# Attention denominators from q's sketch for every chunk but the first, and another queue for the load of S2

## The chip, the cores and the metric

The kernel runs on one core of a Trainium2 chip. The metric is the device time of one execution in microseconds. The engines of the core are called PE (TensorE), DVE (VectorE), ACT (ScalarE), POOL (GpSimd) and SP (SyncE); SP only issues transfers here. Each engine works through its own list of instructions, and waits for the others by semaphores.

## The reference

Two layers follow one another: an attention with a polynomial sketch in place of the softmax, and a feed-forward layer with a squared relu.

```python
def phi(x):                                   # S1, S2: 8 x 32
    a = np.einsum('rd,bhsd->bhsr', S1, x)
    b = np.einsum('rd,bhsd->bhsr', S2, x)
    return np.einsum('bhsi,bhsj->bhsij', a, b).reshape(*x.shape[:-1], 64)
q_p, k_p = phi(q), phi(k)                     # q, k, v: 4 x 4 x 1088 x 32
kv = np.einsum('bhsf,bhsd->bhfd', k_p, v)
z = np.sum(k_p, axis=2)
num = np.einsum('bhsf,bhfd->bhsd', q_p, kv)
den = np.einsum('bhsf,bhf->bhs', q_p, z)[..., None] + 1e-06
x = (num / den)                               # heads side by side: 4352 x 128
h = np.maximum(x @ w_in, 0.0)                 # w_in: 128 x 2048
out = h * h @ w_out                           # w_out: 2048 x 128
```

The denominator is a sum over 64 features of q, but those are products a_i b_j of two sketches of 8 numbers each. So it can be written as the sum over i of a_i times (sum over j of z_ij b_j). The second factor is a sketch of q with its own matrix, S2 weighted by z, of 8 rows again: 8 products in place of 64.

## The kernel before, in words

The work is cut by batch (b = 0 to 3). In each batch, the list `AC` cuts the attention of q into chunks, given as a first group of tokens and a count of groups; batch 0 has three, (0, 8), (8, 12) and (20, 16), and each later batch one. The list `FC` cuts the feed-forward layer into column ranges: 256, 384 and 448 for batch 0. The feed-forward layer runs in units. A unit is one to two blocks of 128 hidden features of one column range: `ffn1` (L610) multiplies x by a block of w_in into the PSUM tile pg, `relu` takes it to SBUF on ACT, `square` squares it on ACT or DVE, and `ffn2` (L637) multiplies by w_out and sums into the PSUM tile po. The first two units hold one block each, the rest of that range two. w_in is rounded on POOL by `cast_wi`, a quarter (four blocks) at a time.

Everything before L815 is the prologue, whose order is the program's own. SP and ACT issue the loads. A DVE transpose of the loaded S1 and S2 (s_nat to s_T, L706) feeds the copies to sf and sq, the sketch matrices. `a_kT0` transposes k, `a_kf` sketches it on PE, `a_kp0` forms the products on DVE, and `a_kv0` sums kv and z on PE into the PSUM tile kvp. The first chunk of q (256 columns) is then made by itself: q0 sketches it into x0, and qp0 is its product. bd is kvp set out in blocks, one half for the denominator and one for the numerator; den0 and num0 are the matmuls with it, and dT, rd, bc and xT on DVE divide one by the other. kvt is a copy of kvp; `a_rep` replicates it by four matmuls with the constant irep, and kv (and z0) are taken from there for the later chunks of batch 0. `keep_warm` issues matmuls whose result isn't used.

Everything after L815 is ordered by a planner, `_Order`. Each task is given its engine, a planned length, a key (a due time) and what it needs; the planner runs through planned time, always taking the ready task of smallest key on a free engine, and writes the instructions out in that order. PSUM has one tile called att for qc, nd, kc and kvp in turn.

For a later chunk, `a_qT` transposes q on DVE, `a_qc` sketches it on PE, `a_qs` spreads the sketches over the features on DVE (qb, qa), `a_qp` multiplies them, `a_nd` multiplies by kv on PE, `a_bc` and `a_x` divide on DVE. Where the denominators come from differs. In batch 0, `a_nd` has further matmuls with z (L547) and `a_dn` turns their rows into reciprocals. In batches 1 to 3, `a_w` (L453) has put the z-weighted sketch matrix into columns 16 to 23 of sw, so `a_qc` yields the weighted sketch beside the others. `a_qt` transposes qc on DVE, `a_pd` multiplies the two sketches, `a_rc` sums and inverts, and `a_rl` moves the results to the partitions that need them by 16 small copies on POOL.

Of the kernel before, what the change touches and what calls it, by code (L numbers as in the profile page):

```python
# [9 lines left out]
F32 = mybir.dt.float32  # L10
# [94 lines left out]
def kernel(  # L105
# [21 lines left out]
    W0, W3 = 10, 3  # L127
# [37 lines left out]
    z0 = sb("z0", 64 * H)  # L165

# [48 lines left out]
    nc.scalar.dma_start(s_nat[8:16, :], S2[:, :])  # L215
# [10 lines left out]
    for p in range(4):  # L226
        load_v(nc.sync, 0, p, 4, NT)
    load_wi(nc.sync, 0)
    load_wi(nc.sync, 1)
    load_q(nc.sync, 0, 256, S)  # L230
# [22 lines left out]
    own_c, own_p = sb("own_c", 32), sb("own_p", 2)  # L253
    nc.vector.memset(own_c[:], 0.0)
# [3 lines left out]
    for h in range(H):  # L258
        nc.vector.memset(own_c[32 * h : 32 * h + 32, 8 * h : 8 * h + 8], 1.0)
# [170 lines left out]
    def a_rep_z(t_, col):  # L430
        nc.vector.tensor_tensor(
            out=_ap(z0, 0, 128, 0, [[32, 4], [128, 2], [1, 32]]),
            in0=_ap(t_, 0, 128, col + 32, [[512, 4], [64, 2], [1, 32]]),
            in1=_ap(own_c, 0, 128, 0, [[0, 4], [0, 2], [1, 32]]),
            op=mult,
        )

# [10 lines left out]
    def a_qc(b, i0, nb):  # L448
        st[b, "qc", i0] = att("qc")
        sketch(st[b, "qc", i0], qT, 32 * i0, 8 * nb, sw[b % 2] if b else sf[:, 64:96])  # L450
# [14 lines left out]
    def a_qt(b, x):  # L465
        if x == 0:
            st[b, "qt"] = wpool.tile([128, 32 * NT * H], F32, tag="qt", bufs=1, name="qt")
        m = 32 * NT
        nc.vector.transpose(  # L469
            _ap(st[b, "qt"], 0, 128, 2 * m * x, [[m, 2], [1, m]]),  # L470
            banks(st[b, "qc", 0], 2 * x, 0, m),
        )

    def a_pd(b):
        qt = st[b, "qt"]
        nc.vector.tensor_tensor(
            out=_ap(pd, 0, 128, 0, [[9, 4 * NT], [1, 8]]),
            in0=_ap(qt, 0, 128, 0, [[32, 4 * NT], [1, 8]]),
            in1=_ap(qt, 0, 128, 16, [[32, 4 * NT], [1, 8]]),
            op=mult,  # L480
        )


    def a_rc(b):
        dn = wpool.tile([128, 4 * NT], F32, tag="dn", name="dn")
        nc.vector.tensor_reduce(
            out=dn[:, :], in_=_ap(pd, 0, 128, 0, [[9, 4 * NT], [1, 9]]), op=add, axis=AX
        )
        st[b, "rc"] = wpool.tile([128, 4 * NT], F32, tag="rc", bufs=1, name="rc")
        nc.vector.reciprocal(st[b, "rc"][:, :], dn[:, :])  # L490


    def a_rl(b, c):
        if c == 0:
            st[b, "rd", 0] = wpool.tile([128, 4 * NT], F32, tag="rd", name="rd")
        for h in range(H):
            nc.gpsimd.tensor_copy(  # L497
                st[b, "rd", 0][32 * h : 32 * h + 32, NT * c : NT * c + NT],
                st[b, "rc"][32 * c : 32 * c + 32, NT * h : NT * h + NT],
            )  # L500
# [26 lines left out]

    def a_nd(b, i0, nb, nd=None, col=0):
        m = 8 * nb
        nd = att("nd") if nd is None else nd  # L530
        st[b, "nd", i0] = nd, col
        kv, z = st[b, "kv"], z0
        for e in range(E):
            qp = st[b, "qp", i0, e]
            ch = [(c, h) for c in range(4) for h in range(H)]
            for c, h in ch:
                r, o = slice(32 * c, 32 * c + 32), 64 * h + 32 * e
                nc.tensor.matmul(  # L538
                    nd[32 * h : 32 * h + 32, 512 * c + col : 512 * c + col + m],
                    kv[r, o : o + 32], qp[r, m * h : m * h + m],  # L540
                    start=(e == 0), stop=(e == 1),
                )
        for o_, m0, w in dens(m) if b == 0 else ():
            for e in range(E):
                for h in range(H):
                    o = 64 * h + 32 * e
                    nc.tensor.matmul(  # L547
                        nd[32 * h : 32 * h + 32, col + o_ : col + o_ + w],
                        z[:, o : o + 32], st[b, "qp", i0, e][:, m * h + m0 : m * h + m0 + w],
                        start=(e == 0), stop=(e == 1),  # L550
                    )

    def dens(m):
        return [(m, 0, m)]

    def a_dn(b, i0, nb):
        m = 8 * nb
        (nd, col), q4 = st[b, "nd", i0], nb // 4
        dT = wpool.tile([128, 32 * NT], F32, tag="dT", bufs=1, name="dT")
        for o_, m0, w in dens(m):  # L560
            nc.vector.transpose(dT[:, m0 : m0 + w], nd[:, col + o_ : col + o_ + w])
        dn = wpool.tile([128, 4 * NT], F32, tag="dn", name="dn")
        nc.vector.tensor_scalar(
            out=_ap(dn, 0, 128, 0, [[q4, 4], [1, q4]]),
            in0=_ap(dT, 0, 128, 0, [[8, 4], [32, q4]]),
            scalar1=1e-6, scalar2=None, op0=add,
        )
        rd = st[b, "rd", i0] = wpool.tile([128, 4 * NT], F32, tag="rd", name="rd")
        nc.vector.reciprocal(rd[:, 0:nb], dn[:, 0:nb])
# [10 lines left out]
    def a_x(b, i0, nb, x, k=2):  # L580
        m = 8 * nb
        if (b, "xT") not in st:
            st[b, "xT"] = bpool.tile([128, SP], F32R, tag="xT", name="xT")
        nc.vector.tensor_tensor(  # L584
            out=_ap(st[b, "xT"], 0, 128, 32 * i0 + 2 * m * x, [[m, k], [1, m]]),
            in0=banks(st[b, "nd", i0][0], 2 * x, st[b, "nd", i0][1], m, k),
            in1=_ap(st[b, "bc", i0], 0, 128, 2 * m * x, [[m, k], [1, m]]),
            op=mult,
        )
# [137 lines left out]
    iden, irep = sb("iden", 128), sb("irep", 128)  # L727
    make_identity(nc, iden[:])
# [27 lines left out]
    a_kf(4, 3, psf, "po")  # L756
    q0(0)
# [3 lines left out]
    for t0, n in ((0, 2), (2, 2), (4, 3), (7, 2)):  # L761
        a_kp0(t0, n)
        for t in range(t0, t0 + n):
            a_kv0(t)
        if t0 == 0:
            a_kf(7, 2, psf, "po")
# [5 lines left out]
    for y in range(2):  # L772
        nc.tensor.matmul(  # L773
            den0[64 * y : 64 * y + 64, 0:256], eps[0:1, 0:64], eps[0:1, 64:320],
            start=True, stop=False,
        )

    bd = sb("bd", 256)
    for x in (1, 0):
# [5 lines left out]
        )  # L785
    st["kvt"] = wpool.tile([128, 128], F32, tag="kvt", name="kvt")
    nc.scalar.copy(st["kvt"][:, :], st[0, "kvp"][:, 0:128])
# [5 lines left out]
    for t_, x in ((den0, 1), (num0, 0)):  # L793
        for y in range(2):
            nc.tensor.matmul(  # L795
                t_[64 * y : 64 * y + 64, 0:256], bd[:, 128 * x + 64 * y : 128 * x + 64 * y + 64],
                qp0[:, 256 * y : 256 * y + 256], start=(x == 0), stop=True,
            )
    a_rep(x0, 256)
    st["warm"] = psf.tile([128, 512], F32, tag="po", name="warm")  # L800
    keep_warm(W3)
    a_rep_kv(x0, 256)
# [10 lines left out]
    a_rep_z(x0, 256)  # L813
# [26 lines left out]
    def q_tasks(b, i0, nb, key):  # L840
# [4 lines left out]
        if True:  # L845
            for x in range(2):
# [7 lines left out]
                )  # L854
        O.add(
            ("qc", b, i0), {"PE": 0.75}, k0 - 1.0, names + [("w", b)], on(a_qc, b, i0, nb),
            rings=[("att", 1)], lag=PEL,
        )
        prev["qTuse"] = [("qc", b, i0)] if i0 + nb == 4 * NT else []
        if b:  # L860
            for x in range(2):
                O.add(
                    ("qt", b, x), {"DVE": dve(m)}, k0 - 0.3 + 0.1 * x, [], on(a_qt, b, x),
                    uses=[("qc", b, i0)], rings=[("qt", 1)] if x == 0 else [],
                )
            O.add(
                ("pd", b), {"DVE": dve(m // 2)}, k0 - 0.1, [("rc", b - 1)], on(a_pd, b),
                uses=[("qt", b, 0), ("qt", b, 1)],
            )
            O.add(  # L870
                ("rc", b), {"DVE": 0.8}, k0 - 0.1, [], on(a_rc, b), uses=[("pd", b)],
                rings=[("rc", 1)],
            )
            for c in range(4):
                O.add(
                    ("rl", b, c), {"POOL": 0.8}, k0 + 0.1 * c, [], on(a_rl, b, c),
                    uses=[("rc", b)], rings=[("rd", 2)] if c == 0 else [],
                )
# [16 lines left out]
    def nd_tasks(b, i0, nb, key):  # L895
# [3 lines left out]
            ("nd", b, i0), {"PE": 1.65 if b else 0.7 + 2.5 * max(nb, 14) / 36}, key - 3.5 - 4 * dve(m), [("kvr", b, h) for h in range(H)], on(a_nd, b, i0, nb),  # L899
            uses=qps + [("qp", b, i0, 0, 0)], rings=[("att", 1)], lag=PEL,  # L900
        )
        if b == 0:
            O.add(
                ("dn", b, i0), {"DVE": 0.72 + m / 960 / 2}, key - 3.0 - 4 * dve(m), [],
                on(a_dn, b, i0, nb), uses=[("nd", b, i0)],
            )
        for x in range(2):
            O.add(
                ("bc", b, i0, x), {"DVE": dve(m)}, key - 2.5 - 4 * dve(m) + 0.1 * x, [], on(a_bc, b, i0, nb, x),
                uses=[("dn", b, i0)] if b == 0 else [("rl", b, 2 * x), ("rl", b, 2 * x + 1)],  # L910
# [88 lines left out]
    for u in range(NU):  # L999
# [8 lines left out]
        for i in range(m):  # L1008
# [13 lines left out]
            tu[u] - 0.6, [],  # L1022
# [65 lines left out]
```

## Time and profile before

| what | value |
|---|---|
| median of 8 runs | 189.24 us (189.12 to 195.46) |
| the profiled execution's own time | 189.18 us |
| its span, first to last instruction | 187.4 us |
| PE busy | 181.8 us, 97% |
| ACT busy | 149.5 us, 80% |
| DVE busy | 114.9 us, 61% |
| POOL busy | 28.0 us, 15% |
| bytes moved | 11.27 MB, mean 60 GB/s |

The profile is that of one execution. Its span is 1.78 us shorter than the time, since something lies before the first instruction and after the last. The busy time of PE includes the time in which a matmul's result is still on its way, so a busy PE need not be full. A line of the timeline has the start in us from the span's begin, the length in us, the engine, the line of the kernel, the operation, its output and inputs, the shape and the count, and in brackets the idle time before it with what ended that. SPq and ACTq are the instructions that issue transfers; PEld are weight loads.

### The profile page before, as it was taken

How to read it: one execution, taken by the hardware profiler on the slowest of the kernel's cores; microseconds unless marked ns; L12 is line 12 of the kernel's file. 1: busy time of each engine (PE TensorE's matmuls, PEld its weight loads, DVE VectorE, ACT ScalarE, POOL GpSimd, SP SyncE). 2: the span in 40 equal slices, each digit the busy share in tenths (PEclk: the TensorE clock that was granted, in tenths of full speed). 3: DMA queues.
4: the chain of work that ended last, by engine and by line, in shares of the span. 5: the costliest groups of instructions: out<-in, count | busy, mean ns of one | idle time of the engine just before them, and what ended most of it. 6: DMA issues, size and time to landing. Idle time of an engine off the chain costs nothing.

```text
span 187.4 us, 4142 instructions
## 1 busy us (share of the span) xinstructions
PE 181.8 (97%) x1586; PEld 121.8 (65%) x1587; DVE 114.9 (61%) x261; ACT 149.5 (80%) x329; POOL 28.0 (15%) x125
## 2 busy tenths in 40 slices
PE   8999999999999999999999999999999999999991
PEld 2757866666656666656577666656577655666890
DVE  4779879958992589469944589469943412222400
ACT  3418778778978989789698989789698998999960
POOL 2841000028400000085000000085000000000000
PEclk9999999999999999999999999999999999999997
DMA  5799600100039600200069200200020200020101
GB/s 184 185 346 305 151 3 2 28 3 5 0 51 242 155 3 0 44 1 2 7 140 257 35 3 0 42 3 0 7 41 0 35 0 2 9 43 0 32 11 28
DMA packets 24411, 11.27 MB, mean 60 GB/s; under 512 B 17864, under 2 KB 22728, under 8 KB 24392
## 3 DMA queue, kind: packets, MB, share of 16 engines
q1 hardware_dynamic: 23940, 10.82, 23.9%
q8 instruction: 12, 0.20, 0.4%
q10 hardware_dynamic: 452, 0.20, 0.4%
q14 instruction: 7, 0.06, 0.1%
HBM read 8.78 MB, written 2.23 MB: 59 GB/s over the span
## 4 chain that ended last, share of the span: by engine, by line
PE 94%; DMA 2%; DVE 1%; issue 0%; ACT 0%; POOL 0%; ACTq 0%; DVEq 0%
PE po L653 60%; PE pg L615 18%; PE nd L538 3%; PE kvp L394 2%; PE pol L648 2%; PE po L648 2%; PE qc L296 2%; DMA s_nat<-in_S_dram 2%; PE kvp L376 1%; PE kf L306 1%; PE kc L296 1%; PE x L749 1%; PE nd L547 1%; PE den L795 0%; PE den L773 0%
## 5 line engine op out<-in xcount | busy, mean ns | idle before, releaser
L653 PE MATMUL po<-g,w_o 128*128 128x384 f32 (+3 forms) x352 | 138.4, 478 | 0.0
L615 PE MATMUL pg<-xT,w_in 128*128 128x384 f32 (+3 forms) x192 | 110.1, 582 | 0.3 <-DVE xT L810 0.3
L624 ACT ACTIVATE gt<-pg 128x384 f32<-128x384 f32 (+4 forms) x177 | 85.3, 490 | 19.9 <-PE pg L615 16.9
L653 PEld LDWEIGHTS po<-g,w_o 128*128 128x128 f32 x352 | 62.6, 189 | 22.3 <-issue 7.3
L632 ACT ACTIVATE g<-gt 128x384 f32<-128x384 f32 (+3 forms) x138 | 71.1, 532 | 2.9
L615 PEld LDWEIGHTS pg<-xT,w_in 128*128 128x128 f32 x192 | 36.0, 190 | 25.1 <-issue 6.0
L634 DVE TENSOR_TENSOR g<-gt 128x384 f32<-128x384 f32 (+4 forms) x39 | 21.3, 549 | 39.5 <-ACT gt L624 39.4
L443 POOL COPY kv<-kvt 32x64 f32<-32x64 f32 x48 | 11.8, 246 | 90.5 <-PE po L653 63.9
L506 DVE STREAM_SHUFFLE qa<-qc 128x576 f32<-128x576 f32 (+2 forms) x20 | 11.6, 653 | 0.0
L521 DVE TENSOR_TENSOR qp<-qa,qb 128x576 f32<-128x576 f32 (+2 forms) x20 | 10.8, 607 | 0.0
L497 POOL COPY rd<-rc 32x9 f32<-32x9 f32 x48 | 8.9, 185 | 2.1
L347 DVE TENSOR_TENSOR kp<-fs 128x576 f32<-128x576 f32 x12 | 8.2, 739 | 0.0
L469 DVE STREAM_TRANSPOSE qt<-qc 128x576 f32<-128x576 f32 x6 | 4.3, 761 | 5.6 <-PE qc L296 5.6
L657 DVE STREAM_TRANSPOSE oT<-po 128x384 f32<-128x384 f32 (+3 forms) x11 | 6.2, 562 | 1.2 <-PE po L653 1.0
L538 PE MATMUL nd<-qp,kv 32*32 32x288 f32 (+2 forms) x320 | 6.8, 353 | 0.0
L338 DVE STREAM_TRANSPOSE fs<-kc 128x576 f32<-128x576 f32 x6 | 4.3, 761 | 3.9 <-PE kc L296 3.9
L538 PEld LDWEIGHTS nd<-qp,kv 32*32 32x32 f32 x320 | 3.8, 103 | 3.5 <-issue 2.1
L584 DVE TENSOR_TENSOR xT<-nd,bc 128x576 fp32r<-128x576 f32 (+2 forms) x10 | 5.6, 596 | 0.8 <-PE nd L538 0.7
L506 DVE STREAM_SHUFFLE qb<-qc 128x576 f32<-128x576 f32 (+2 forms) x10 | 6.0, 647 | 0.0
L289 DVE STREAM_TRANSPOSE qT<-qn 128x192 f32<-128x192 f32 (+3 forms) x11 | 5.8, 561 | 0.0
L696 PE MATMUL warm<-const-bfloat16-1.0 128*128 128x512 bf16 x12 | 4.9, 561 | 0.8 <-PEq L1072 0.8
L575 DVE STREAM_TRANSPOSE bc<-rd 128x576 f32<-128x576 f32 (+2 forms) x10 | 5.7, 609 | 0.1
(98 smaller groups left out, 97.6 us busy)
## 6 DMA issues: line engine op xcount, KB each, us to landing
kn<-in_k_dram SPq DMA_DIRECT2D x3, 544.0 KB, 7.0
qn<-in_q_dram SPq DMA_DIRECT2D x3, 544.0 KB, 7.0
vn<-in_v_dram SPq DMA_DIRECT2D x9, 144.0 KB, 5.7
out_dram<-oT SPq DMA_DIRECT2D x24, 48.0 KB, 1.8
w_in<-in_moe_w_in_dram SPq DMA_DIRECT2D x4, 256.0 KB, 5.4
w_o<-in_moe_w_out_dram SPq DMA_DIRECT2D x4, 256.0 KB, 5.2
out_dram<-oT SPq DMA_DIRECT2D x8, 56.0 KB, 1.9
qn<-in_q_dram SPq DMA_DIRECT2D x1, 416.0 KB, 4.8
```

The lines of the kernel that those rows point to most:

```text
L347: nc.vector.tensor_tensor(out=_ap(st[b, "kp"], 0, 128, 2 * o, [[64, NT], [8, 8], [1, 8]]), in0=_ap(fs, 0, 128, o, [[32, NT], [1, 8], [0, 8]]),
L443: nc.gpsimd.tensor_copy(_ap(st[b, "kv"], 32 * c, 32, 64 * h, [[32, E], [1, 32]]), _ap(st["kvt"], 32 * h, 32, 0, [[64, E], [1, 32]]),)
L497: nc.gpsimd.tensor_copy(st[b, "rd", 0][32 * h : 32 * h + 32, NT * c : NT * c + NT], st[b, "rc"][32 * c : 32 * c + 32, NT * h : NT * h + NT],)
L506: nc.vector.stream_shuffle(in_=banks(st[b, "qc", i0], 2 * x, 0, m), out=_ap(st[b, which, i0], 0, 128, 2 * m * x, [[m, 2], [1, m]]), mask=m ...
L521: nc.vector.tensor_tensor(out=st[b, "qp", i0, e][:, r], in0=st[b, f"qa{e}", i0][:, r], in1=st[b, "qb", i0][:, r], op=mult,)
L538: nc.tensor.matmul(nd[32 * h : 32 * h + 32, 512 * c + col : 512 * c + col + m], kv[r, o : o + 32], qp[r, m * h : m * h + m], start=(e == 0 ...
L615: nc.tensor.matmul(st["pg", u][:, n * i : n * i + n], w_in[:, 128 * (d0 + i) : 128 * (d0 + i) + 128], st[b, "xT"][:, c0 : c0 + n],)
L624: nc.scalar.activation(gt[:, 0:w], st["pg", u][:, 0:w], Relu)
L632: nc.scalar.activation(g2[:, 0:w], gt[:, 0:w], Square)
L634: nc.vector.tensor_tensor(out=g2[:, 0:w], in0=gt[:, 0:w], in1=gt[:, 0:w], op=mult)
L648: nc.tensor.matmul(po[x // 128][:, 0:128], g[:, x : x + 128], w, start=(d == 0), stop=(d == NB - 1),)
L653: nc.tensor.matmul(po[0][:, 0:n], w, g, start=(d == 0), stop=(d == NB - 1))
```

## The change

It has these parts.

- The denominators of batch 0's second and third chunks are made as those of batches 1 to 3 are. The matmuls with z, `a_dn`, `a_rep_z`, z0 and own_c go. `a_qt`, `a_pd`, `a_rc` and `a_rl` take the chunk's first group and count, and the planner gives these tasks to every chunk after the first.
- The weighted sketch matrix of batch 0 is made in the prologue: own_f is a mask summed from the identity, zm is z with that mask, s2f is S2 transposed, and four small matmuls give columns 16 to 23 of sw, which ACT copies out of x0.
- The sketch qc of the second chunk, and its two transposes of q, go from the planner into the prologue; the load of q is cut at column 640, and its first part stands ahead of w_in's.
- S2 is the first load on SP's queue; S1 alone stays on ACT's.
- The last of the four sketches of k comes before the kv matmuls and not between them; kvt is copied by DVE; the replicas come before num0; the identity is made earlier on POOL. The matmuls of `keep_warm` there are one and one, not three.
- The squares of the first two units have an earlier due time.

```diff
-    W0, W3 = 10, 3
+    W0, W3, W4 = 10, 1, 1
...
     nc.scalar.dma_start(s_nat[0:8, :], S1[:, :])
-    nc.scalar.dma_start(s_nat[8:16, :], S2[:, :])
+    nc.sync.dma_start(s_nat[8:16, :], S2[:, :])
     load_k(nc.sync, 0, 0, 512)
...
         load_v(nc.sync, 0, p, 4, NT)
+    load_q(nc.sync, 0, 256, 640)
     load_wi(nc.sync, 0)
     load_wi(nc.sync, 1)
-    load_q(nc.sync, 0, 256, S)
+    load_q(nc.sync, 0, 640, S)
...
+    iden, irep = sb("iden", 128), sb("irep", 128)
+    make_identity(nc, iden[:])
+
+    own_f, s2f, zm = sb("own_f", 16), sb("s2f", 32), sb("zm", 32)
+    nc.vector.tensor_reduce(
+        out=own_f[:, :], in_=_ap(iden, 0, 128, 0, [[8, 16], [1, 8]]), op=add, axis=AX
+    )
...
-        sketch(st[b, "qc", i0], qT, 32 * i0, 8 * nb, sw[b % 2] if b else sf[:, 64:96])
+        sketch(st[b, "qc", i0], qT, 32 * i0, 8 * nb, sw[b % 2])
...
-        for o_, m0, w in dens(m) if b == 0 else ():
-            for e in range(E):
-                for h in range(H):
-                    o = 64 * h + 32 * e
-                    nc.tensor.matmul(
-                        nd[32 * h : 32 * h + 32, col + o_ : col + o_ + w],
-                        z[:, o : o + 32], st[b, "qp", i0, e][:, m * h + m0 : m * h + m0 + w],
-                        start=(e == 0), stop=(e == 1),
-                    )
...
     a_kf(4, 3, psf, "po")
+    a_kf(7, 2, psf, "pg")
     q0(0)
     q0(1)
...
-        if t0 == 0:
-            a_kf(7, 2, psf, "po")
+
+    nc.vector.transpose(s2f[:, :], _ap(sf, 0, 128, 72, [[0, 4], [1, 8]]))
...
+    for i0 in (8, 14):
+        a_qT(0, i0, 6)
...
+    a_bd(1)
     st["kvt"] = wpool.tile([128, 128], F32, tag="kvt", name="kvt")
-    nc.scalar.copy(st["kvt"][:, :], st[0, "kvp"][:, 0:128])
+    nc.vector.tensor_copy(st["kvt"][:, :], st[0, "kvp"][:, 0:128])
+
+    nc.vector.tensor_tensor(
+        out=_ap(zm, 0, 128, 0, [[16, 2], [8, 2], [1, 8]]),
+        in0=_ap(st[0, "kvp"], 0, 128, 32, [[64, 2], [0, 2], [1, 8]]),
+        in1=_ap(own_f, 0, 128, 0, [[0, 2], [8, 2], [1, 8]]),
+        op=mult,
+    )
+    a_bd(0)
...
+    nd0(den0, 1)
+    for h in range(H):
+        nc.tensor.matmul(
+            x0[32 * h : 32 * h + 32, 384:392], s2f[:, :], zm[:, 8 * h : 8 * h + 8],
+            skip_group_check=True,
+        )
     a_rep(x0, 256)
+    nc.scalar.copy(sw[0][:, 16:24], x0[:, 384:392])
+    a_rep_kv(x0, 256)
+    nd0(num0, 0)
     st["warm"] = psf.tile([128, 512], F32, tag="po", name="warm")
     keep_warm(W3)
-    a_rep_kv(x0, 256)
+    a_qc(0, *AC[0][1])
+    keep_warm(W4)
...
-    a_rep_z(x0, 256)
...
-        if b:
-            for x in range(2):
...
+        for x in range(2):
+            O.add(
+                ("qt", b, i0, x), {"DVE": dve(m)}, k0 - 0.3 + 0.1 * x, [], on(a_qt, b, i0, nb, x),
+                uses=[("qc", b, i0)], rings=[("qt", 1)] if x == 0 else [],
+            )
...
+        for c in range(4):
+            O.add(
+                ("rl", b, i0, c), {"POOL": 0.8}, k0 + 0.1 * c, [], on(a_rl, b, i0, nb, c),
+                uses=[("rc", b, i0)], rings=[("rd", 2)] if c == 0 else [],
+            )
...
-            tu[u] - 0.6, [],
+            tu[u] - (0.6 if u > 1 else 40.0), [],
```

In the planned order that results, chunk 1's pd stands ahead of the first two squares on DVE and its dn and rc behind them; POOL's cast of the last quarter of w_in stands behind that chunk's 16 copies rd; and nd, kc, qc and kvp of chunk 2 and of batch 1 move past one or two matmuls of the feed-forward layer.

## The prediction, made before the changed kernel was run

> **What bounds the kernel now.** I read the page's busy shares and chain, then the timeline of the first 46 us instruction by instruction, since the diff acts there only. TensorE (PE) is busy 97% of the 187.4 us span and carries 94% of the chain of work that ended last:
>
> ```profile
> PE 181.8 (97%) x1586; PEld 121.8 (65%) x1587; DVE 114.9 (61%) x261; ACT 149.5 (80%) x329; POOL 28.0 (15%) x125
> ...
> PE 94%; DMA 2%; DVE 1%; issue 0%; ACT 0%; POOL 0%; ACTq 0%; DVEq 0%
> ```
>
> A saving on PE counts only where PE is the bound. The timeline (start, length, engine, line) shows where that is:
>
> ```profile
> 0.73 0.89 SPq L173 DMA_DIRECT2D kn<-in_k_dram  x2
> ...
> 0.92 0.59 ACTq L214 DMA_DIRECT2D s_nat<-in_S_dram  x1
> ...
> 1.53 0.29 ACTq L215 DMA_DIRECT2D s_nat<-in_S_dram  x1
> ...
> 3.50 0.71 DVE L283 STREAM_TRANSPOSE kt<-kn 128x512 f32<-128x512 f32 x1 [1.20 <-DMA kn<-in_k_dram]
> ...
> 4.50 0.20 DVE L706 STREAM_TRANSPOSE s_T<-s_nat 32x32 f32<-32x32 f32 x1 [0.29 <-DMA s_nat<-in_S_dram]
> ...
> 5.30 1.75 PE L306 MATMUL kf<-sf,kt 128*128 128x64 f32 x14 [0.37 <-ACT sq L717]
> ...
> 8.66 0.66 PE L306 MATMUL kf<-sf,kt 128*128 128x64 f32 x4
> ...
> 11.15 0.49 DVE L780 TENSOR_TENSOR bd<-kvp,own_p 128x128 f32<-128x128 f32 x2 [0.26 <-PE kvp L376]
> ...
> 12.31 0.45 DVE L804 STREAM_TRANSPOSE dT<-den 128x256 f32<-128x256 f32 x1 [0.67 <-PE den L795]
> ...
> 13.58 0.42 DVE L810 TENSOR_TENSOR xT<-num,bc 128x256 fp32r<-128x256 f32 x1
> ...
> 14.15 0.71 PE L615 MATMUL pg<-xT,w_in 128*128 128x256 f32 x4 [0.27 <-DVE xT L810]
> ...
> 14.79 0.59 PE L296 MATMUL qc<-qT,sf 32*32 32x96 f32 x32
> ...
> 16.26 1.07 ACT L624 ACTIVATE gt<-pg 128x512 f32<-128x512 f32 x2
> ...
> 16.98 0.48 PE L615 MATMUL pg<-xT,w_in 128*128 128x256 f32 x2
> ...
> 18.92 0.96 PE L538 MATMUL nd<-qp,kv 32*32 32x96 f32 x64
> ...
> 19.81 0.54 PE L547 MATMUL nd<-qp,z 128*32 128x96 f32 x16
> ...
> 20.28 0.39 PE L615 MATMUL pg<-xT,w_in 128*128 128x256 f32 x1
> ...
> 34.49 0.65 PE L547 MATMUL nd<-qp,z 128*32 128x128 f32 x16
> ...
> 45.65 3.59 POOL L497 COPY rd<-rc 32x9 f32<-32x9 f32 x16
> ```
>
> Four stages follow. To 5.3 the bound is the arrival of S and k. From 5.3 to 11.1 PE streams. From 11.15 to 14.15 it is a DVE chain (bd, dT, rd, bc, xT). From 14.5 to about 17 it is ACT: the unit at 16.98 needs the relu that began at 16.26 behind an unbroken ACT run. From 17.3 PE is packed to the end; one 256-column pg plus its po repeats every 0.55 us.
>
> **What the Trainium skill says.** "Perfetto Trace Analysis", DMA Instruction — HWDGE: the descriptor generator is shared and locked, and the profiled length includes the wait for the lock. The trace fits: S1 took 0.59 beside SP's k load, S2 alone 0.29. Same page, GPSIMD Engine Instruction: time GpSimd by start-to-start spacing; here 3.59/16 = 0.224 us against a reported 0.184. "TensorE: Matmul & The Clock Gate", Architectural detail: the queues of VectorE and ScalarE are strict first-in first-out, GpSimd's per core; nothing in the trace runs out of order there. Same page, "Wait — 56ns, not 53.3ns?": starts of matmuls are never under about 25 ns apart; kvp with its weights goes at 1.71/56 = 30.5 ns, while the 32*32 tiles, which share the array, go faster (64 in 0.89).
>
> **The change, part by part.**
>
> *S2 on SP's queue.* S2 must wait for the memset of s_nat (0.80 to 0.89), so it issues at 0.92 on SP, and both k loads, q and v stand behind it. Price: 0.29 (its length alone) to 0.59 (with the lock), so the first k load moves from 0.73 to 1.25..1.55, and k lands at 3.43 + 0.52..0.82 = 3.95..4.25. s_T stands behind the transpose of that k: 3.95..4.25 + 0.07 + 0.64 (0.71 less 0.07 overlap, as between L283's later two) = 4.66..4.96, against 4.50 now. S2 no longer ends last; k does. PE starts 0.16..0.46 later; I take 0.30, since S1 takes the lock at the same moment.
>
> *a_kf(7,2) ahead of kvp.* No work goes, but PE changes shape twice less: 8.66 to 9.25 held 0.59 for four, where 4 x 0.125 = 0.50 is the pace of the first fourteen, and kvp's first 16 took 0.62 where the later pace gives 0.49. Saved 0.2. kvp's PSUM buffer is now kf(2,2)'s, free when DVE's second kp ends near 7.6 (+0.3), before PE gets there at 8.8.
>
> *DVE before bd.* s2f (0.20, like s_T), qp, and two qT (0.62 for both, L289) now precede bd(1). qp waits for qb: x ends 0.5 later than now plus the 0.3, so qb 9.0 to 9.6, qp to 10.3, qT to 10.9; kvp ends at 11.1 + 0.3 - 0.2 = 11.2. Hidden with 0.3 to spare, if q's 192 KB have landed by 10.6. They issue near 6.4 where w_in's first 256 KB issued at 5.96 and landed 3.9 later: an estimate of 9.9 to 10.3. Without that cover every us of lateness is a us of the chain.
>
> *The chain to the first pg.* den starts at bd(1) + 0.46 and dT 0.70 after den, as now. kvt's copy (0.27 on ACT now) and zm (0.2) fit between the two bd. On PE, from den's start: den 0.43, eight small zm products 0.2 to 0.45 (25 to 56 ns each), replicas 0.45, num 0.43, making 1.75 at most, against 1.97 until xT needs num. Then warm 0.21, qc 0.52, warm 0.21: 2.6 after den's start, where pg could start at 2.54 (14.15 - 11.61). qc must also wait for ACT's kv copy out of the same PSUM tile (0.37); sw's copy (0.2, as zero_a's) runs under the replicas. So pg keeps its distance, give or take 0.1. First pg: 14.15 + 0.30 - 0.20 = 14.25.
>
> *qc out of the ACT stage.* 0.52 leaves PE between 14.8 and 15.4, but ACT's run starts from the first pg and is unchanged; the next pg waits for the relu anyway. Worth 0. z (0.41) and two qT leave DVE; qt x2 (0.7) and pd (0.3) take their place, so the first two squares keep within 0.15, and po has that much slack.
>
> *Denominators off PE.* L547 goes: 20.28 - 19.81 = 0.47 at chunk 1, 35.07 - 34.49 = 0.58 at chunk 2. Both lie where PE is packed: 1.05 in all. dT, dn, rd on DVE (0.68 and 0.73) go too; qt, pd, dn, rc (about 1.5 each) come, ahead of qb. qp of chunk 1 then ends 4.9 after the first pg, at 19.1, where PE arrives at 19.0: about 0.1 of wait.
>
> *The cast of w_in's last quarter.* It stands on POOL behind chunk 1's 16 rl copies; it ran at 15.87 to 16.49. From the first pg: both relus and squares end at +1.55, dn (0.26, between the 0.22 of 64 and the 0.49 of 324 elements) at +1.8, rc (0.23) at +2.05; 16 copies of 32x3 at 0.217 (0.224 for 9 elements less 6 at the 1.1 ns by which the 64-element copies differ) = 3.5 to +5.6; cast 0.62 to +6.2; hop: +6.3, so 20.5. The matmul behind nd needs that quarter. It starts at 20.28 now and would start near 19.95 without the wait: 0.5 of stall, less or more by 0.3. Below nothing is excluded: it waits or it doesn't. So chunk 1 brings no gain: 20.5 - 20.28 = 0.2 lost, the 0.05 of the prologue in it.
>
> *The rest.* Chunk 2: qt to rc delay its qp by 1.2, but nd moves back one and a half pg/po pairs of 0.82 in PE's order; PE at 34.2, qp ready 33.9. Its rl end near 32.5, before bc. kvp(1) needs ks only for its last eight matmuls. Other exchanges of neighbours move whole pieces past packed PE work: 0.
>
> Sum against the profiled execution: +0.2 - 0.58 = -0.4; span 187.0. Around the span lie 189.18 - 187.4 = 1.78: 188.8. That execution stands 0.06 under the median of 189.24.
>
> **Rivals.**
>
> *Both savings arrive.* If rl runs faster than its spacing, or PE reaches that pg later than I think, the cast is in time: 0.05 - 1.05 = -1.0, 188.2. For: the stall is a difference of two sums six us long. Against: POOL's order is fixed, 16 copies then the cast.
>
> *No net gain.* k slips by the full 0.82 (PE 0.46 later) and the stall is 0.8: +0.5 - 0.58 = -0.1, 189.1. For: the lock. Against: nothing in particular.
>
> *Slower: the q load stalls DVE.* qT waits at the head of DVE's queue, with bd, den, dT and xT behind it. Now q's second load lands at 6.83 + 4.8 = 11.6. If the new piece shares the rings and lands there rather than near 10.1, the chain moves by 11.6 - 10.6 = 1.0: 189.8. It decides from 11.4 on (0.4 + 0.4 beyond 10.6). For: DMA is 0.9 busy from 9 us. Against: it is 192 KB and ahead of w_in.
>
> *S2 does not hold k back*, since generation overlaps: start no later than now, -0.7, 188.5; this sits within the forecast's range.
>
> **How the numbers follow.** Forecast 0.50 (188.5 to 189.05), both savings 0.27, no gain 0.11, q late 0.12. A measurement of this kernel can tell 0.2%, 0.38 us: under 188.86 is faster, over 189.62 slower. The forecast's half splits 0.28 to 0.22. Faster 0.28 + 0.27 = 0.55, same 0.22 + 0.11 = 0.33, slower 0.12. The range takes in most of the second case, and the third, and leaves out the worst of the fourth: 188.15 to 189.4.
>
> **What would show it.** s_T starts at 4.7 to 4.9 with the k transposes just ahead of it; kvp runs unbroken; qT on DVE shows no DMA wait; the first pg near 14.25; POOL's cast right after 16 rl copies, ending near 20.4, and pg waiting for it; no z products; chunk 2's nd without a wait. A pg at 19.9 after nd, or a DVE wait for q's DMA, proves the sum wrong.

## The result: 191.4 us, slower, and outside the range

| | kernel before | changed kernel |
|---|---|---|
| median | 189.2 us (32 runs) | 191.4 us (11 runs) |
| lowest and highest | 189.03 to 195.53 | 189.67 to 193.28 |
| ratio, 95% interval | | 1.010, 1.0085 to 1.0116 |
| profiled execution: time, span | 189.18, 187.4 | 193.29, 191.5 |
| POOL busy in it | 28.0 us | 36.2 us |

The forecast was 188.8 in a range of 188.15 to 189.4. The ratio leaves out executions more than 1.5% above the fastest of their kernel; with them the spread of the changed kernel is in four groups, and that is part of the finding: 189.67 (once), 191.23 to 191.44 (seven times), 192.9 to 193.0 (twice), and 193.28 (once; the profiled one, 193.29, is like it).

The page of the changed kernel, in parts 1, 2 and 4, has these rows:

```profile
PE 184.0 (96%) x1561; PEld 123.8 (65%) x1562; DVE 117.1 (61%) x264; ACT 148.9 (78%) x328; POOL 36.2 (19%) x157
...
PEclk9999999999999999999999999999999999999999
...
PE 91%; POOL 2%; DMA 2%; DVE 1%; issue 1%; SPq 0%; ACT 0%; POOLq 0%
```

PE has 25 instructions fewer and is busy 2.2 us longer. POOL, with 0% of the chain of work that ended last before, has 2% of it. So two things happened: PE's instructions took longer, and PE waited for POOL. The timeline has both. Its lines are those that the prediction showed of before:

```profile
0.77 4.42 PE L662 MATMUL warm<-const-bfloat16-1.0 128*128 128x512 bf16 x10 [0.77 <-PEq L1058]
...
0.91 0.41 SPq L213 DMA_DIRECT2D s_nat<-in_S_dram  x1
...
1.38 0.85 SPq L171 DMA_DIRECT2D kn<-in_k_dram  x2
...
4.48 0.71 DVE L286 STREAM_TRANSPOSE kt<-kn 128x512 f32<-128x512 f32 x1 [1.93 <-DMA kn<-in_k_dram]
...
5.12 0.16 DVE L672 STREAM_TRANSPOSE s_T<-s_nat 32x32 f32<-32x32 f32 x1
...
5.88 4.07 PE L309 MATMUL kf<-sf,kt 128*128 128x64 f32 x18 [0.68 <-ACT sq L683]
...
9.88 2.08 PE L713 MATMUL x<-qT,sq 64*128 64x256 f32 x8
...
13.23 0.63 DVE L292 STREAM_TRANSPOSE qT<-qn 128x192 f32<-128x192 f32 x2
...
14.93 0.29 DVE L748 TENSOR_TENSOR bd<-kvp,own_p 128x128 f32<-128x128 f32 x1 [1.07 <-PE kvp L379]
...
17.93 0.79 PE L581 MATMUL pg<-xT,w_in 128*128 128x256 f32 x4
...
20.23 4.25 POOL L492 COPY rd<-rc 32x3 f32<-32x3 f32 x16 [4.70 <-DVE rc L484]
...
22.78 0.96 PE L531 MATMUL nd<-qp,kv 32*32 32x96 f32 x64
...
24.55 0.61 POOL L655 CAST w_in<-w_in 128x512 fp32r<-128x512 f32 x1
...
25.21 0.38 PE L581 MATMUL pg<-xT,w_in 128*128 128x256 f32 x1 [1.46 <-POOL w_in L655]
...
39.40 1.07 PE L531 MATMUL nd<-qp,kv 32*32 32x128 f32 x64
```

Read it in three steps.

*k is late.* S2's issue (0.41) stands ahead of the k loads, which go at 1.38 in place of 0.73. k reaches DVE at 4.48, 0.98 later than before; s_T runs at 5.12 (4.50), and kf starts at 5.88 (5.30).

*PE runs at about half pace.* Two lines of the kernel before, to compare:

```profile
0.77 4.17 PE L696 MATMUL warm<-const-bfloat16-1.0 128*128 128x512 bf16 x10 [0.77 <-PEq L1072]
...
6.98 1.14 PE L749 MATMUL x<-qT,sq 64*128 64x256 f32 x8
```

Before, 14 kf took 1.75 us, 0.125 each. Here 18 took 4.07, 0.226 each; x took 2.08, not 1.14. So bd, at 11.15 before, comes at 14.93. From bd to the first pg it is 3.00 in both kernels. The warm-up differs too: ten matmuls took 4.17 before, since the last of them ran faster, and 4.42 here.

*PE waits for the cast.* From the first pg to the matmul behind nd it is 7.28 us (25.21 - 17.93), against 6.13 before (20.28 - 14.15), though the products with z are gone. The 16 copies rd took 4.25, the cast stands behind them, and PE waits 1.46.

The half pace is not in every execution, so the late k, the half pace and the wait had to be taken apart on the chip.

### The profile page after: what moved, and what is told of

Its sections match the earlier page's. It is cut to its first block, busy times and chain, and to the rows that moved or that the text cites. A ratio compares the mean times of both kernels' runs of the same rounds, so it can differ in the third digit from the quotient of the medians.

```text
span 191.5 us, 4132 instructions
## 1 busy us (share of the span) xinstructions
PE 184.0 (96%) x1561; PEld 123.8 (65%) x1562; DVE 117.1 (61%) x264; ACT 148.9 (78%) x328; POOL 36.2 (19%) x157
## 4 chain that ended last, share of the span: by engine, by line
PE 91%; POOL 2%; DMA 2%; DVE 1%; issue 1%; SPq 0%; ACT 0%; POOLq 0%
PE po L619 57%; PE pg L581 16%; PE nd L531 3%; PE kf L309 2%; PE kvp L397 2%; POOL rd L492 2%; PE pol L614 2%; PE po L614 2%; PE qc L299 2%; DMA kn<-in_k_dram 2%; PE kvp L379 2%; PE kc L299 1%; PE x L713 1%; DVE qt L464 0%; POOL w_in L655 0%
## 5 line engine op out<-in xcount | busy, mean ns | idle before, releaser
L600 DVE TENSOR_TENSOR g<-gt 128x384 f32<-128x384 f32 (+4 forms) x40 | 22.0, 553 | 39.9 <-ACT gt L590 39.9
L492 POOL COPY rd<-rc 32x9 f32<-32x9 f32 (+2 forms) x80 | 17.0, 213 | 17.2 <-DVE rc L484 13.8
L464 DVE STREAM_TRANSPOSE qt<-qc 128x576 f32<-128x576 f32 (+2 forms) x10 | 5.8, 615 | 6.2 <-PE qc L299 6.1
L614 PE MATMUL pol<-w_o,g 128*128 128x128 f32 x32 | 5.7, 275 | 0.0
```

The costliest lines, as they stand in the source:

```text
L492: nc.gpsimd.tensor_copy(st[b, "rd", i0][32 * h : 32 * h + 32, n * c : n * c + n], st["rc"][32 * c : 32 * c + 32, n * h : n * h + n],)
L600: nc.vector.tensor_tensor(out=g2[:, 0:w], in0=gt[:, 0:w], in1=gt[:, 0:w], op=mult)
L614: nc.tensor.matmul(po[x // 128][:, 0:128], g[:, x : x + 128], w, start=(d == 0), stop=(d == NB - 1),)
```

## The experiments

Where a kernel was run several times, the number that tells most is the count of executions in each group, so it is collected in a table behind the experiments.

### 1. What slows PE in the prologue: the late k, or the idle time?

Two more warm-up matmuls in the changed kernel:

```diff
-    W0, W3, W4 = 10, 1, 1
+    W0, W3, W4 = 12, 1, 1
```

> The changed kernel with 12 warm-up matmuls at the start instead of 10, nothing else. Theory (half pace after a gap): in the changed kernel PE has nothing to do between the last warm-up matmul and the first k sketch for 0.68 us, against 0.37 before, and then runs at half pace until 13.3; two more matmuls of 0.43 fill the gap. The k sketches then take 0.125 us each again (18 in 2.25), the first pg comes 8.65 after the first k sketch, near 14.7, and the time is about 190.1. Rival (the half pace comes from the order of the work or from the late k itself): the k sketches keep 0.226 us each and the time stays above 191.

Measured: 189.87 us median (189.75 to 191.68, 9 runs), ratio 1.005 (1.0021 to 1.008). Timeline of this kernel:

```profile
0.77 4.46 PE L662 MATMUL warm<-const-bfloat16-1.0 128*128 128x512 bf16 x12 [0.77 <-PEq L1058]
...
5.86 2.19 PE L309 MATMUL kf<-sf,kt 128*128 128x64 f32 x18 [0.62 <-ACT sq L683]
...
11.41 0.29 DVE L748 TENSOR_TENSOR bd<-kvp,own_p 128x128 f32<-128x128 f32 x1 [0.40 <-PE kvp L379]
...
14.41 0.80 PE L581 MATMUL pg<-xT,w_in 128*128 128x256 f32 x4
...
16.82 4.25 POOL L492 COPY rd<-rc 32x3 f32<-32x3 f32 x16 [1.28 <-DVE rc L484]
...
21.14 0.61 POOL L655 CAST w_in<-w_in 128x512 fp32r<-128x512 f32 x1
...
21.80 0.38 PE L581 MATMUL pg<-xT,w_in 128*128 128x256 f32 x1 [1.57 <-POOL w_in L655]
```

k is as late, kf starts at 5.86 (5.88 in the changed kernel), and its 18 take 2.19: the late k by itself doesn't slow PE. The expectation had the time and the pace right, but not the way to them: the idle 0.62 is still there in this execution, since twelve took scarcely longer than ten had (4.46 against 4.42), as the last of them ran at full pace. The pace had come up before the idle time began.

The other way round: the kernel before, with k in time, and two warm-up matmuls fewer.

```diff
-    W0, W3 = 10, 3
+    W0, W3 = 8, 3
```

> The kernel before with 8 warm-up matmuls instead of 10, no part of the change. The first k sketch stays at 5.3, so that only the gap before it grows, by two matmuls of 0.43 to about 1.2. Theory (the gap alone is enough): half pace in the k sketches and the time at 190.5 to 193. Rival (the late loads cause it): no difference, 189.2.

Measured: 192.32 us median (190.67 to 194.21, 4 runs), ratio 1.0126 (1.0061 to 1.0191). Its timeline, PE alone:

```profile
5.26 3.22 PE L306 MATMUL kf<-sf,kt 128*128 128x64 f32 x14 [0.92 <-ACT sq L717]
8.41 2.08 PE L749 MATMUL x<-qT,sq 64*128 64x256 f32 x8
```

With nothing of the change in it, and k in time, kf runs at 0.23 each. So PE can stay at half pace without the late k and without the new order. This run doesn't tell the longer idle time from the shorter warm-up, all of which ran at the slow pace (eight in 3.57). The runs with ten warm-up matmuls do that better: that with S2 moved in section 2, and section 4.

### 2. S2 on each queue, without the rest

S2 back on ScalarE's queue in the changed kernel:

```diff
-    nc.sync.dma_start(s_nat[8:16, :], S2[:, :])
+    nc.scalar.dma_start(s_nat[8:16, :], S2[:, :])
```

> The changed kernel with S2's load back on ScalarE's queue, nothing else undone. Theory: k lands near 3.4 again, the first k sketch starts near 5.3, the gap is 0.37 again and PE keeps its full pace; the first pg is near 14.0, the matmul behind the second chunk's numerators still waits 1 us or more for POOL's cast, and the time is 189.0 to 189.5. Rival (the order of the prologue costs the pace): half pace in the k sketches again, time above 190.5.

Measured: 189.61 us median (189.18 to 192.98, 20 runs), ratio 1.0034 (1.0011 to 1.0056). The median is just above the expected range, which had no stretch at half clock behind the wait. The profiled execution, of 190.84 us, has kf at 5.27 and the first pg at 13.82, 0.33 ahead of before. It also shows what the middle group of this kernel is. PE's timeline, from the wait on:

```profile
21.11 0.38 PE L581 MATMUL pg<-xT,w_in 128*128 128x256 f32 x1 [1.47 <-POOL w_in L655]
21.33 0.64 PE L619 MATMUL po<-g,w_o 128*128 128x256 f32 x2
...
22.48 0.78 PE L581 MATMUL pg<-xT,w_in 128*128 128x256 f32 x1
23.05 1.06 PE L619 MATMUL po<-g,w_o 128*128 128x256 f32 x2
```

and its table of stretches (after the stretch and the core's granted clock come DMA's share and GB/s):

```profile
21.00:22.00 1.00, 0.89 (x5) 0.84 (x6) 1.00 (x5) 0.00 (x0) 0.06 (x1) 0.88 0.91 196
22.00:23.00 1.00, 1.00 (x4) 0.82 (x4) 1.00 (x2) 0.75 (x2) 0.00 (x0) 0.50 0.40 143
23.00:24.00 1.00, 1.00 (x5) 0.82 (x4) 0.16 (x1) 0.48 (x1) 0.00 (x0) 0.50 0.04 17
24.00:25.00 1.00, 1.00 (x5) 0.82 (x4) 0.01 (x1) 0.60 (x1) 0.00 (x0) 0.50 0.00 0
25.00:26.00 1.00, 1.00 (x6) 0.81 (x4) 0.68 (x1) 0.53 (x2) 0.00 (x0) 0.92 0.00 0
```

The first number after the range is its length; the last but two is PE's granted clock. It falls to 0.50 within a us of the wait's end and stays there until about 25.1, and a pg takes 0.78, not 0.47. Half the clock for some 3.4 us goes with about 1.6 of time: the seven executions of this kernel at 190.84 to 191.03 (mean clock 0.99) stand that much above the eleven at 189.18 to 189.7 (medians 190.91 and 189.32).

S2 on SyncE's queue and nothing else, in the kernel before:

```diff
-    nc.scalar.dma_start(s_nat[8:16, :], S2[:, :])
+    nc.sync.dma_start(s_nat[8:16, :], S2[:, :])
```

> The kernel before with S2 as the first load of SP's queue, nothing else of the change. Theory: the first k sketch moves from 5.3 to about 5.9, the gap to about 0.7, PE runs at half pace for several us, and the time is 191 to 193. Rival (the queue costs only its delay): 189.2 + 0.6 = 189.8.

Measured: 189.74 us median (189.43 to 194.81, 20 runs), ratio 1.0038 (1.0019 to 1.0056). PE's timeline of an execution of the lowest group:

```profile
0.77 4.43 PE L696 MATMUL warm<-const-bfloat16-1.0 128*128 128x512 bf16 x10 [0.77 <-PEq L1072]
...
5.86 1.75 PE L306 MATMUL kf<-sf,kt 128*128 128x64 f32 x14 [0.66 <-ACT sq L717]
```

kf starts at 5.86 (0.66 idle) and the first pg at 14.70, against 14.15: the move costs 0.46 in the executions without a halved clock (the median of the 11 lowest is 189.66). It also brings the gap, and nine of 20 lie above 191, where the kernel before, run beside it, had five of 44 above 190. So the move alone makes such executions common, though not the rule: here kf runs at full pace behind the gap. By the median the rival's 189.8 was right, and the theory's 191 to 193 came in a part of the executions only. Three of the nine have a mean clock of 0.99, and this kernel has no wait for the cast: a stretch at half clock can come without that wait.

### 3. The cast

In the changed kernel, an earlier due time for the cast of w_in's last quarter, which puts it ahead of the 16 copies on POOL:

```diff
-    ND, QT, WI, KL, QL = 2, 3.0, (1.5, 3.0), (30.0, 12.0), 4.0
+    ND, QT, WI, KL, QL = 2, 3.0, (1.5, 1.5), (30.0, 12.0), 4.0
```

> The changed kernel with the planned earliest time of the cast of w_in's last quarter set from 3.0 to 1.5, so that POOL makes it before chunk 1's 16 copies; S2 stays on SP's queue. Theory (the matmul behind chunk 1's numerators waits 1.15 us for that cast, and PE's clock is halved for 3.4 us after that wait in most executions): neither the wait nor the half clock at that place is left, granted clock 0.997 or more in most executions, time 188.5 to 188.9. Rival (chunk 1's copies, now behind the cast, make xT the next wait): 189.3 or more.

Measured: 189.69 us median (188.27 to 192.02, 12 runs), ratio 0.9995 (0.9971 to 1.002). The cast is at 16.28, the matmul behind nd has no wait, and the lowest group falls from 189.67 (one execution) to 188.27..189.31 (six). Executions at a mean clock of 0.99 are two of 12, where the changed kernel has seven of 13. The median is above the expected 188.5 to 188.9, because executions at 191.8 to 192.0 remain, with S2 still on SyncE's queue. The profiled one (190.2 us of span) is one with the prologue at half pace:

```profile
5.71 4.07 PE L309 MATMUL kf<-sf,kt 128*128 128x64 f32 x18 [0.51 <-ACT sq L683]
9.71 2.08 PE L713 MATMUL x<-qT,sq 64*128 64x256 f32 x8
```

Does a wait for the cast halve the clock by itself? The kernel before, with 30 idle copies on POOL ahead of that cast:

```diff
     def cast_wi(c):
+        for i in range(30 if c == 3 else 0):
+            r0, r1 = 32 * (i % 4), 32 * (i // 4 % 4)
+            nc.gpsimd.tensor_copy(dmy[r0 : r0 + 32, 0:3], sf[r1 : r1 + 32, 64:67])
```

> The kernel before with 30 idle copies of 32x3 on POOL ahead of the cast of w_in's last quarter, and nothing of the change. Theory: the cast ends near 21.5, the matmul behind chunk 1's numerators waits about 1.3 us, base time 190.5, and in a good part of the executions the granted clock is halved for 3.4 us after that wait, 1.65 us more: 192.1, clock 0.99. Rival (the half clock belongs to the changed prologue): all executions near 190.5. The copies that run beside a two-input DVE operation should last as long as that, the others 0.22 us apart.

Measured: 194.87 us median (193.23 to 195.49, 4 runs), ratio 1.0288 (1.0232 to 1.0345). POOL's timeline:

```profile
15.41 7.97 POOL L692 COPY dmy<-sf 32x3 f32<-32x3 f32 x30
23.45 0.61 POOL L693 CAST w_in<-w_in 128x512 fp32r<-128x512 f32 x1
```

and PE's, behind nd:

```profile
24.11 0.58 PE L616 MATMUL pg<-xT,w_in 128*128 128x256 f32 x1 [3.77 <-POOL w_in L693]
24.49 1.05 PE L654 MATMUL po<-g,w_o 128*128 128x256 f32 x2
24.98 0.78 PE L616 MATMUL pg<-xT,w_in 128*128 128x256 f32 x1
```

and two of its stretches of half a us (the last but two is again the granted clock):

```profile
21.50:22.00 0.50, 0.00 (x0) 0.81 0.38 132
...
28.50:29.00 0.50, 0.50 (x4) 0.86 0.00 0
```

The wait was mis-sized: 3.77, where about 1.3 was meant, since a copy takes 0.266 (7.97/30) and each was charged at less. In a kernel without any of the change, a wait for the cast is followed by pg at 0.78 and po at 1.05 until about 28.6, so the half clock doesn't need the changed prologue. The clock fell inside the wait, at about 21.8, and was half for 6.8 us. For a wait of 1.5 us this says nothing: that rests on the kernel with S2 back. The median doesn't help either. Two of the four executions (194.44 and 195.49) stand where four of the 17 of the kernel before stood beside them (194.34 to 195.42).

### 4. What the products with z were worth

The kernel before without those matmuls, its denominators read from the numerators' rows:

```diff
-        for o_, m0, w in dens(m) if b == 0 else ():
+        for o_, m0, w in ():
...
-            nc.vector.transpose(dT[:, m0 : m0 + w], nd[:, col + o_ : col + o_ + w])
+            nc.vector.transpose(dT[:, m0 : m0 + w], nd[:, col : col + w])
```

> The kernel before without its z matmuls; the denominators are read from numerator rows, so that part of the computation is left out. All else stands. Theory (PE packed there): 1.05 us less, 188.15. Rival (DVE or ACT bounds these stretches): 188.7 to 189.2.

Measured: 188.46 us median (187.98 to 188.65, 5 runs), ratio 0.9953 (0.9937 to 0.997): 0.73 by the medians, 1.06 by the lowest times (187.98 against 189.04). The profiled execution is one of 188.65:

```profile
0.78 4.42 PE L696 MATMUL warm<-const-bfloat16-1.0 128*128 128x512 bf16 x10 [0.78 <-PEq L1072]
...
5.24 2.27 PE L306 MATMUL kf<-sf,kt 128*128 128x64 f32 x14
...
14.61 0.72 PE L615 MATMUL pg<-xT,w_in 128*128 128x256 f32 x4 [0.27 <-DVE xT L810]
...
20.27 0.38 PE L615 MATMUL pg<-xT,w_in 128*128 128x256 f32 x1
```

There kf's 14 took 2.27, not 1.75, and the first pg came 0.46 later than before. From the first pg to the matmul behind chunk 1's nd it is 5.66, against 6.13, and to that behind chunk 2's nd 19.88 (34.49 - 14.61), against 20.92 (35.07 - 14.15): 1.04 saved. So the 1.05 that the prediction took was there to be had.

The same profile shows what the idle time does. The warm-up ran at the slow pace, as in the changed kernel (4.42 in both), but kf followed without a gap, and PE was at full pace within kf. Behind the gap of 0.68 it stayed slow for all of kf and x. These are single executions, though; what carries the claim is the table of groups.

### 5. The copies on POOL

In the changed kernel, memsets of the same shape in place of the 16 copies:

```diff
-            nc.gpsimd.tensor_copy(
+            nc.gpsimd.memset(
                 st[b, "rd", i0][32 * h : 32 * h + 32, n * c : n * c + n],
-                st["rc"][32 * c : 32 * c + 32, n * h : n * h + n],
+                1.0 + c
             )
```

> The changed kernel with memsets of the same shape in the place of the 16 small copies rd of POOL (left out: the distribution of the denominators; x is wrong by them). If POOL's copies are held up because they read SBUF while a DVE instruction with two SBUF inputs runs, no memset is held up: the 16 take the same spacing in chunk 1 as in batches 1 to 3, under 0.2 us each and none above 0.3; they end at about +3 from their start, the cast about 1 us earlier, PE's wait for it falls from 1.46 to under 0.6. If POOL slows for another reason (its queue, the semaphores at each copy), single memsets are as long as the long copies, 0.5 to 0.75. If 1.46 us is what halves the clock and a wait under 0.6 doesn't, hardly any execution shows a granted clock of 0.99: median 189.2 or less.

Measured: 191.52 us median (189.76 to 191.67, 4 runs), ratio 1.01 (1.0065 to 1.0135). What the view of the tile rd tells of the changed kernel between 20 and 25 us (after the count: the shortest, median and longest in ns):

```profile
L492 POOL COPY rd<-rc x16: 175/182/599, 20.2 to 24.3; 32x3 f32<-32x3 f32 x16
```

and of this kernel, over the whole span:

```profile
L492 POOL MEMSET rd<- x80: 90/97/103, 15.5 to 130.8; 32x9 f32 x48, 32x3 f32 x16, 32x4 f32 x16
```

A copy is 182 ns in the median, but one takes 599. It starts at 23.2, beside a square on DVE (23.12 to 23.77) with two inputs from SBUF; of the copies beside the products qp (from 21.75) the longest takes 375. The Trainium skill, "SBUF — State Buffer", Who interferes with whom, says that such a DVE instruction and a GpSimd instruction that reads SBUF exclude one another for a whole instruction, and that one that only writes is free. That fits: no memset is over 103 ns, though pd and two squares on DVE (18.58 to 19.52) ran beside the second sixteen (18.17 to 20.25). But the memsets don't wait for rc, so they also ran earlier than the copies do; the lock is likely and not shown apart from that.

In the profiled execution there is no wait for the cast, and PE's clock was not halved behind nd. Yet no execution came at 189.2 or below, against the expectation: three stand at 191.5 to 191.7, of which the profiled one has the prologue at half pace (kf 0.58 idle, then 18 in 4.07), and one at 189.76 has a mean clock of 0.991. Removing the wait alone leaves the gap ahead of kf.

### 6. The changed kernel once more

For a profile of its typical execution, with no edit:

> The changed kernel once more, for a profile of its typical execution. If that is one stretch of halved PE clock behind the wait for POOL's cast: time about 191.3, granted clock about 0.99; kf from 5.88 with its 18 in 2.2, kvp in 2.3, bd near 11.4, first pg near 14.4, the wait for w_in near 1.5, and then pg at 0.78 and po at 1.06 each for some 3.4 us. If the typical execution is one with a slow prologue: kf's 18 in 4.07 and bd near 14.9, and nothing behind the wait.

Measured: 193.11 us (192.91 and 193.3). The profiled one was again one with the prologue at half pace (kf 0.74 idle, 18 in 4.07). So no profile of the changed kernel itself at 191.3 exists; that this group has one stretch at half clock rests on its mean clock of 0.99, its distance of 1.65 from 189.67, and the profile of the kernel with S2 back.

### 7. A version without either idle stretch

The change with S2 on ScalarE's queue, eleven warm-up matmuls, the earlier cast, and the last quarter of w_in loaded earlier:

```diff
-    W0, W3, W4 = 10, 1, 1
-    ND, QT, WI, KL, QL = 2, 3.0, (1.5, 3.0), (30.0, 12.0), 4.0
+    W0, W3, W4 = 11, 1, 1
+    ND, QT, WI, KL, QL = 2, 3.0, (1.5, 1.5), (30.0, 12.0), 4.0
...
-    nc.sync.dma_start(s_nat[8:16, :], S2[:, :])
+    nc.scalar.dma_start(s_nat[8:16, :], S2[:, :])
...
-    load_wo(nc.sync, 1)
     load_wi(nc.sync, 3)
+    load_wo(nc.sync, 1)
```

> The same, with S2's load back on ScalarE's queue, w_in's last quarter loaded ahead of w_out's second, and 11 warm-up matmuls. Theory: what is left is the shorter prologue (first pg 13.8 against 14.15) and the 1.05 us of z products, with 0.2 us lost near the second chunk's k work: 188.0 to 188.3. Rival (xT of chunk 1 comes late): 188.8.

> The best version so far (the change, S2 on ScalarE's queue, the last quarter of w_in loaded ahead of the second half of w_out and cast ahead of the 16 copies, eleven warm-up matmuls), in more executions: 188.1 to 188.7, ratio to the kernel before 0.995 to 0.997, none with a granted clock of 0.99.

Measured: 188.37 us median (188.1 to 188.62, 4 runs), ratio 0.9958 (0.9942 to 0.9974), and then 188.5 (188.01 to 192.1, 6 runs), ratio 0.9958 (0.9943 to 0.9972). It beats the kernel before by 0.4%, and the changed one by more. PE's timeline of the second:

```profile
5.42 2.18 PE L309 MATMUL kf<-sf,kt 128*128 128x64 f32 x18
...
13.96 0.80 PE L581 MATMUL pg<-xT,w_in 128*128 128x256 f32 x4
...
19.61 0.96 PE L531 MATMUL nd<-qp,kv 32*32 32x96 f32 x64
20.50 0.38 PE L581 MATMUL pg<-xT,w_in 128*128 128x256 f32 x1
```

No idle time stands ahead of kf, and none behind nd. Nine of its ten executions are at 188.01 to 188.65; one, not profiled, is at 192.1, so it isn't free of executions above 190. And it isn't the eleventh warm-up matmul alone that does it. In the kernel before:

```diff
-    W0, W3 = 10, 3
+    W0, W3 = 11, 3
```

> The kernel before with eleven warm-up matmuls in place of ten. If that is all that the best version has over the kernel before: 188.5. If the extra matmul only closes the 0.37 us gap in front of kf, which seldom cost anything there: 189.1 to 189.3, no difference, but fewer executions at 195.

Measured: 189.36 us median (189.09 to 189.88, 22 runs), ratio 1.0008 (1.0001 to 1.0015): no gain, but also no execution over 190. The kernel before, run beside it, has two of 27 above 194 (and five of 32 beside the changed kernel), so 22 are too few to show that the eleventh prevents them.

### All executions by group

"One stretch" is some 1.4 to 1.8 us above the lowest group, at a mean clock of about 0.99; "more" lies higher: by the mean clock two such stretches (about 0.98, none of them profiled), or, by the profiles of those that were profiled, a prologue at half pace. The idle times are those of the profiled execution. Where no execution is in the lowest group, the others are assigned by their mean clock. The row of the changed kernel leaves out its first profiled execution (193.29). The kernel with idle copies is not in it, since its wait of 3.77 moves all groups.

| kernel | idle ahead of kf | wait for the cast | lowest group | one stretch | more |
|---|---|---|---|---|---|
| before | 0.37 | none | 27 | 0 | 5 |
| before, 8 warm-up | 0.92 | none | 0 | 1 | 3 |
| before, 11 warm-up | 0.41 | none | 22 | 0 | 0 |
| before, S2 on SyncE's | 0.66 | none | 11 | 3 | 6 |
| changed, early cast | 0.51 | none | 6 | 2 | 4 |
| changed, memsets | 0.58 | none | 0 | 1 | 3 |
| changed, 12 warm-up | 0.62 | 1.57 | 7 | 2 | 0 |
| changed, S2 on ScalarE's | 0.26 | 1.47 | 11 | 7 | 2 |
| changed, all its runs | 0.68 | 1.46 | 1 | 7 | 5 |
| the version of 7 | none | none | 9 | 0 | 1 |

Either idle stretch goes with a spoiled part of the executions. With k in time, one stretch comes in seven of 20 with the wait for the cast, and in none of 64 with full warm-up and without that wait (before, 11 warm-up, the version of 7). The changed kernel has both idle stretches, and 12 of 13 of its executions are spoiled. The counts favour the wait for the cast as the source of its typical stretch (seven of 13 with it, two of 12 with the early cast), but such stretches also come where only the gap ahead of kf stands (three of 20 with S2 moved in the kernel before), and no execution of that group was profiled: which of the two it is in the changed kernel stays open.

## Why the prediction was wrong, point by point

The forecast was 188.8, -0.4. The one execution without any halved clock is at 189.67, which is +0.47 (seven of the kernel with twelve warm-up matmuls, at 189.75 to 189.96, bear it out), and the median is at 191.4. So of the 2.6 missed, 0.9 come from two terms that were mis-sized, S2's move and the wait for the cast; they alone turned the sign. The other 1.7 come from a term that the prediction put at nothing without a reason: what PE's clock does around an idle stretch.

- **PE's clock** is the larger part, and no step of the prediction has it. It showed PE idle for 0.37 ahead of kf, had PE start later, and priced this and the stall behind nd at their length alone. The stretch of half clock costs about 1.6 in the kernel with S2 back, more than the wait of 1.47 ahead of it. The Trainium skill, "TensorE: Matmul & The Clock Gate", What's actually happening, has the two clocks and a window of about 3.4 us that runs freely. The length of the slow stretch there (about 21.76 to 25.16) and the change from one execution to the next agree with it. The prediction cited this page for other things.
- **"S2 on SP's queue"** had the mechanism and not the size. The issue was priced rightly: k's load went 0.65 later, inside 0.52 to 0.82. But it then took 3.08 to land and not 2.7, and k at DVE was +0.98. Why it took longer is not shown; with S2 gone from ScalarE's queue, two loads of v are issued there at 1.60 to 2.42, beside k's, where before they were at 1.92 and 3.50. kf started 0.58 later; 0.30 was taken and 0.46 was the upper end. End to end it is 0.46 in the kernel before. One reading of the trace was wrong as well: S2's 0.29 was not that of an issue alone, since SP's loads ran until 1.62 and from 1.66 beside it (1.53 to 1.82). On SP beside S1 it was 0.41.
- **"The cast of w_in's last quarter"** named the wait and its place, and was 1 us short. Predicted 0.5 of stall, measured 1.46. In the execution at full pace with twelve warm-up matmuls, the copies start 2.41 after the first pg and not 2.05 (16.82 - 14.41), and take 4.25, not 3.5: sixteen times 0.266. The 0.217 came from copies of batches 1 to 3, where the longest of batch 1 is 189 ns and DVE ran only shuffles beside them. The two terms, 0.36 and 0.75, are the missing 1.1. Most of the 0.36 is the first two squares, which were to keep within 0.15: they start 1.16 after the first pg (15.57), where before it was 0.81 (14.96), since qt waited 0.34 for qc on PE. PE's arrival was right: nd ended 5.8 after the first pg, 5.7 predicted.
- **"Denominators off PE"** was right: z's matmuls are gone, chunk 2's nd at 39.40 has no wait, and the products are worth 1.04 in the trace of section 4.
- **"The chain to the first pg"** was right to 0.1: 3.00 from bd in both. First pg 14.41 in an execution at full pace, 14.25 predicted; the difference is the late k. The prologue's net is +0.10 by this sum (0.30 - 0.20), and 0.05 where the prediction uses it later; the slip decides nothing.
- **"DVE before bd"** was right: qT shows no wait for q's load, at full pace too (10.38 with twelve warm-up matmuls). The rival that ended slower rested on that wait, and did not happen; it was slower for another reason.
- **"a_kf(7,2) ahead of kvp"** was right in sign: with S2 on ScalarE's queue the first pg is 0.33 earlier, where 0.2 was taken.
- **The rivals.** "No net gain", with k late and a longer stall, is the nearest to the lowest group: it had 189.1 for a stall of 0.8, and 189.67 came with 1.46. "Both savings arrive" is excluded by the wait for the cast, and "S2 does not hold k back" by k at 4.48.
- **The signs to look for** that failed: s_T at 5.12 for 4.7 to 4.9, and the cast's end at 21.75 for 20.4 (the execution with twelve).

The account of the lowest group, +0.47: S2 is 0.35 of it (189.67 less 189.32, the median of the 11 lowest with S2 back), or 0.46 as measured in the kernel before. The rest of the change is then +0.12 (189.32 less 189.2). In the trace of the kernel with S2 back, the prologue's -0.33 and chunk 1's longer way to the matmul behind nd (7.29 for 6.13, +1.16), with chunk 2's -0.58 from the row of before, make +0.25. The 0.13 between the two is unresolved.

## What to carry to other kernels

Price an idle stretch of PE not at its length alone, but also at what the clock does after it: where PE was packed, a stall of one and a half us cost double in some executions, so look at the groups of times and not at one profile. Count the filler matmuls ahead of a load so that at the slow pace (0.44 us each here) they last until that load is used; where they sped up sooner, the gap that was left did no harm. Before work is put on a lightly used engine, look at what stands behind it in that engine's queue, and take the copy's duration from a stretch in which the other engines are as busy.

## What the runs showed of the hardware that was not expected

- A wait of 1.47 us on PE was followed by half clock for about 3.4 us in the kernel with S2 back. By the mean clock this was so in seven of its 20 executions, and with twelve warm-up matmuls and a wait of 1.57 in two of nine. The Trainium skill, "TensorE: Matmul & The Clock Gate", Why this matters for your kernels, warns of gaps above about 3 us; here half of that was enough. The measurement decides.
- At the start, PE stayed at half pace until 13 to 16 us behind gaps of 0.51 to 0.92 us ahead of kf, where the warm-up matmuls had all run at the slow pace (ten in 4.42 or 4.43, eight in 3.57): so in five of six such profiles. The exception is the kernel before with S2 moved (0.66 idle, then 14 in 1.75). With the same warm-up and no gap (section 4), PE was at full pace within kf. Where the warm-up had sped up before its end (ten in 4.17, 4.23 or 4.27; twelve in 4.46), idle times of 0.25 to 0.62 did no harm.
- The row of the granted clock reads 9 all through the profile of the changed kernel, though kf took 0.226 each. It shows the later halved stretch in the kernel with S2 back, as 8 in the slices concerned, but not a slow start: there, compare the duration of one matmul with a known one.
- A POOL copy of 32 x 3 was 182 ns in the median and up to 599 beside DVE's work, and sixteen took 4.25 us and not the 3.5 estimated.
